# An attention and feed-forward kernel: an FFN step's activation one step later, weight loads behind queries, two banks for the values' products

## The chip, the cores and the metric

The kernel runs on one core of a Trainium2 chip. A core has five engines with queues of their own: TensorE (PE: matmuls, and PEld, the loading of the stationary operand), VectorE (DVE), ScalarE (ACT), GpSimd (POOL) and SyncE (SP, which only issues transfers here). Each engine takes its instructions in order and waits on semaphores. The metric is the device time of one execution in microseconds; the span in a profile is the time from the first to the last instruction of one profiled execution.

## The reference

```python
# q, k, v: 8 batches x 8 heads x 576 positions x 64
scores = scale * np.matmul(q, k.transpose(0, 1, 3, 2))
# heads 0..3: the last 32 positions; heads 4..7: equal position modulo 32, causal
scores = np.where(masks, scores, -1e9)
attn = np.exp(scores - scores.max(-1)); attn = attn / (attn.sum(-1) + 1e-9)
x = np.matmul(attn, v)           # regrouped to 4608 tokens x 512
h = x @ w_in                     # 512 x 2048
g = h * (1.0 / (1.0 + np.exp(-1.702 * h)))
return g @ w_out                 # 2048 x 512
```

## The kernel before

**Attention** goes in 48 pairs of blocks (`pairs`, l.50-71), four heads each. A pair's work: `scores` (PE), `maxima` (DVE), `softmax` (eight exponentials on ACT, the reciprocal of the sums on DVE, the scaling on POOL), a transposition, `values` (16 products on PE into one PSUM bank, then a high part by ACT and a low part by DVE, the tiles xh and xl). The first ten pairs (`n0`) are done ahead of the FFN in the loop of l.550-578; its turns are called stages here. Stage i has, in program order: scores(i+1) on PE, the load of q and k for pair i+3, the reciprocal of pair i-1, the fetch of the transposed pair i-2, the low part of pair i-3 and the maxima of pair i+1 on DVE, the exponentials of pair i on ACT, values(i-2) on PE with its high part on ACT, and PE's transposition of pair i-1. For these ten pairs all values' products go to one bank, `first_a` (l.145, l.293).

**The FFN** goes in 12 groups of 384 tokens and 16 slices f of 128 hidden units: 192 steps (`steps`, l.527), ordered (group 0, f 0-7), (group 1, f 0-15), (group 0, f 8-15), and then group by group. Step s has on PE `ffn1` (12 matmuls of 384 columns into a bank h), and at its end `ffn2` of step s-2 (9 matmuls of 512 columns into three banks o). Between them stands `act` (l.461): tanh on ACT, the product with h on DVE (both tile g), the high part gh on ACT, the low part gl on DVE. `ffn1` and `ffn2` take three products each, high x high, high x low and low x high, so that a weight's high and low parts are both needed.

**The weights** come as 64-bit words and are taken apart once, by a generator (`weights`, l.401); `weigh(n)` runs it until n turns, called beats here, have been issued. Per slice f of the weights: ACT scales the upper words (in the trace raw<-raw, f32) and makes the lower ones (raw<-raw, uint8), DVE joins them (raw<-raw, uint32); ACT then takes the high part (w<-raw) and DVE the low part (w<-raw,w). Beat 5+3f issues the joining of slice f+1 and the high part of f; beat 6+3f the low part of f, the load of slice f+4, and the scaling of f+2; beat 7+3f the lower words of f+2. The first four slices are loaded by explicit calls of `load_w`, two transfers of 512 KB each (l.533, l.554). Step s needs beats 5+3s and 6+3s.

**What sets the order.** PE keeps program order throughout. ACT, DVE, POOL and SP keep it as long as `strict` holds (l.600): until all 51 beats are issued, at step 21. After that a planner orders them by what is ready. PSUM has two banks for scores (`s`) and six for everything else (`x`, l.88): in the first stage four for scores and transpositions and one for the values, later three o, the banks h and one for values' products.

Of the kernel before, what the change touches and what calls it, by code (L numbers as in the profile page):

```python
# [43 lines left out]
LAG = 2  # L44
RAWB = 4
NH = NF // 2
WEIGHED = 6


def _pairs():  # L50

    def strided(b):
        return [("s", b, c) for c in range(0, len(RES), U)]

    def local(j):
        n = G // QL
        return [("l", i // NL, i % NL) for i in range(j * n, (j + 1) * n, U)]

    def weave(a, b):
        return [u for i in range(max(len(a), len(b))) for u in a[i : i + 1] + b[i : i + 1]]

    first = {}
    for b in range(B):
        first.setdefault(b * S // G, []).extend(strided(b))
    ahead = local(0) + first[0]
    windows = [weave(first.get(j + 1, []), local(j + 1)) for j in range(NG - 1)] + [[]]
    ahead += windows[0]
    windows[0] = []  # L70
    return ahead + [u for w in windows for u in w], windows, len(ahead)
# [3 lines left out]
def attn_ffn(ctx, tc, qk, vs, w_in, w_out, masks, ident, out):  # L75
# [11 lines left out]
    def bank(name):  # L87
        tag, n = ("s", 2) if name[0] == "s" else ("x", 6)
        return psum.tile([P, 512], F32, tag=tag, name=name, bufs=n)
# [7 lines left out]
    pairs, windows, n0 = _pairs()  # L97
# [32 lines left out]
    def load_v(p):  # L130
        if p < len(pairs) and p not in vts:
            vts[p] = io.tile([P, U, HEADS, D], F32, tag="v", name=f"v_{p}", bufs=2)
            sync.dma_start(out=vts[p], in_=vs[p])
# [8 lines left out]


    first = [[bank(f"{x}{j}") for j in range(2)] for x in "sut"]
    first_a = bank("a")


    prs = [const.tile([P, HU, P], F32, name=f"pr_{i}") for i in range(AHEAD)]
# [7 lines left out]
    def geom(p):  # L156

        kind, b, c = pairs[p]
        if kind == "l" and c == 0:
            m = masks_sb[:QL, 0:U].rearrange("p u n -> p (u n)")  # L160
            return QL, KL, m.unsqueeze(1).broadcast_to([QL, 2, U * KL])
        n, nk, i = (QL, KL, 1) if kind == "l" else (RES[c] * NPOS, RES[c] * NPOS, 2)
        return n, nk, masks_sb[:n, i, :nk].unsqueeze(1).broadcast_to([n, 2 * U, nk])
# [124 lines left out]
    def values(p):  # L288

        kind, b, c = pairs[p]  # L290
        nq, nk, _ = geom(p)
        v, pt = vts[p], pts[kind]
        ops = first_a if p < n0 else bank(f"a_{p}")
        for u in range(U):
            for g in range(2):
                for j in range(2):
                    i = g * U + u
                    matmul(
                        ops[j * D : (j + 1) * D, i * nq : (i + 1) * nq],
                        lhsT=v[:nk, u, 2 * g + j, :],  # L300
                        rhs=pt[:nk, j * 2 * U + i, :nq],
                        start=True,
                        stop=True,
                    )
        parts = []
        if kind == "l":
            j, o = divmod((NL * b + c) * QL, G)
            src = ops[:, : 2 * U * nq].rearrange("p (g n) -> p g n", g=2)
            parts.append([src] + [x[:, :, o : o + U * QL] for x in part("l", j)])
        else:  # L310
            n, r0 = U * RES[c], R0[c]
            src = ops[:, : 2 * U * nq].rearrange("p (g r t) -> p g t r", g=2, r=n)
            t0 = 0
            while t0 < NPOS:
                j, o = divmod(NPOS * b + t0, G // STRIDE)
                t1 = min(NPOS, t0 + G // STRIDE - o)
                xv = [x.rearrange("p c (t r) -> p c t r", r=STRIDE) for x in part("s", j)]
                parts.append(
                    [src[:, :, t0:t1]] + [x[:, :, o : o + t1 - t0, r0 : r0 + n] for x in xv]
                )  # L320
                t0 = t1
        yield
        for src, hi, _ in parts:
            scalar.copy(out=hi, in_=src)
        yield
        for src, hi, lo in parts:
            vector.tensor_tensor(out=lo, in0=src, in1=hi.bitcast(F32), op=ALU.subtract)
# [5 lines left out]
    def w_tile(shape, dtype, name):  # L333
        return wp.tile(shape, dtype, tag="w", name=name, bufs=NF)

    def load_w(f):

        if f >= NF:
            return
        raw = raws[f] = w_tile([P, 2, DM, 2], U32, f"raw_{f}")  # L340
        for m in range(2):
            sync.dma_start(out=raw[:, m], in_=(w_in, w_out)[m][f])
# [95 lines left out]
    made = [0]  # L438

    def weigh(n):  # L440

        while made[0] < n and next(wgen, 0) is None:
            made[0] += 1
# [17 lines left out]
    def act(j, f, beside=lambda: None):  # L461
        ps = hps.pop((j, f))
        g2 = ffn.tile([P, G], F32, tag="g2", name=f"g2_{j}_{f}", bufs=1)
        scalar.activation(g2, ps[:, :G], AF.Tanh, scale=0.851)
        vector.scalar_tensor_tensor(
            out=g2, in0=g2, scalar=1.0, in1=ps[:, :G], op0=ALU.add, op1=ALU.mult
        )
        beside()
        gh, gl = (
            ffn.tile([P, G], F32R, tag=f"g{x}", name=f"g{x}_{j}_{f}", bufs=LAG + 1) for x in "hl"  # L470
        )
        scalar.copy(out=gh, in_=g2)
        vector.tensor_tensor(out=gl, in0=g2, in1=gh.bitcast(F32), op=ALU.subtract)
        gs[j, f] = (gh, gl)
# [53 lines left out]
    steps = [(j, f) for j, f0, f1 in spans for f in range(f0, f1)]  # L528
# [1 line left out]
    load_v(0)  # L530
    ident_sb = const.tile([P, P], F32, name="ident_sb")
    sync.dma_start(out=ident_sb, in_=ident)
    load_w(0)
    scores(0)
    maxima(0)
    load_qk(2)
    load_v(1)
    halfway, valued = {}, {}

    def scaled(p):  # L540
        run(halfway.pop(p))
# [8 lines left out]
    for i in range(n0):  # L550
        if i + 1 < n0:
            scores(i + 1)
            load_qk(i + 3)
        if i + 1 < RAWB:
            load_w(i + 1)
        if i >= 1:
            scaled(i - 1)
        if i >= 2:
            fetch_pt(i - 2)
        if i >= 3:  # L560
            late_part(i - 3)
        if i + 1 < n0:
            maxima(i + 1)
        halfway[i] = softmax(i)
        run(halfway[i], 4)
        if i >= 2:
            value_products(i - 2)
            load_v(i)
            run(valued[i - 2], 1)
        weigh(i)  # L570
        if i == n0 - 2:
            turn_pr(i - 1)
            ffn1(*steps[0], (0, 1))
        elif i == n0 - 1:
            ffn1(*steps[0], (2, 3))
            turn_pr(i - 1)
        elif i >= 1:
            turn_pr(i - 1)
# [6 lines left out]
    p = n0  # L585
# [13 lines left out]
    for s in range(len(steps) + LAG):  # L599
        strict[0] = made[0] < 3 * NF + 3  # L600
        cur = steps[s] if s < len(steps) else None
        old = steps[s - LAG] if s >= LAG else None
        p, q, r = due.get(s), due.get(s - 1), begins.get(s)
        if cur:
            if s == 1:
                scaled(n0 - 1)
                fetch_pt(n0 - 2)
                late_part(n0 - 3)
            if s == 2:
                fetch_pt(n0 - 1)  # L610
                late_part(n0 - 2)
            if s > 0:
                ffn1(*cur, range(NC))
            if s in (1, 2):
                value_products(n0 - 3 + s)
            if s == 1:
                turn_pr(n0 - 1)
                act(*steps[0], lambda: weigh(made[0] + 1))
            goal = WEIGHED + min(3 * (s + 1), 3 * NH + (s + 1 - NH) * 3 // 2)
            if s > 0:  # L620
                act(*cur, lambda: weigh(min(made[0] + 1, goal)))
            if s in (1, 2):
                run(valued[n0 - 3 + s], 1)
            weigh(goal)
            if s == 2:
                late_part(n0 - 1)
        if late is not None:
            run(late[0], -(-4 // (late[1] - s)) if late[1] > s else HU)
        if p is not None:
            load_v(p)  # L630
            load_qk(p + AHEAD)
            transpose(p)
        if q is not None:
            run(values(q))
            load_v(q + 1)
        if r is not None:
            scores(r)
            maxima(r)
            load_qk(r + 1)
            if late is not None:  # L640
                run(late[0])
            late = softmax(r), turn[r]
            run(late[0], 1)
        if old:
            for parts in ((0, 1, 2),) if old[1] == NF - 1 else ((0, 1), (2,)):
                for i in range(NT):
                    ffn2(*old, i, parts)
            gs.pop(old)
# [77 lines left out]
```

## Time and profile before

| | us |
|---|---|
| median of three runs | 962.55 (960.97 to 963.12) |
| the profiled execution | 961.34 |
| its span | 959.6 |
| PE busy | 930.5 |
| DVE busy | 523.3 |
| ACT busy | 408.7 |

Two runs of the same kernel differ here by up to 2.2 us. In the views below a row of the timeline has start, duration, engine, line, operation, tiles out<-in and the shapes; in square brackets stands how long the engine sat idle before it and what ended that. All work is issued through one helper, so every line is L108, and one goes by tile names: s, u scores; t transposed; a values' products; h, o, g, gh, gl the FFN; raw, w the weights; qk, v queries with keys, and values.

### The profile page before, as it was taken

What the parts mean: (1) busy time and instruction counts of PE and PEld (TensorE: products, weight loads), DVE (VectorE), ACT (ScalarE), POOL (GpSimd) and SP (SyncE); (2) the same over time, 40 slices, a digit from 0 to 9 for tenths busy, and PEclk for the clock granted to TensorE, in tenths of its full rate; (3) what the DMA queues carried; (4) which work ended last, traced back from release to release, by engine and by line L of the source; (5) the groups of instructions that cost most, each with busy time, mean ns of one, the idle gap of its engine ahead of it and who ended that gap; (6) DMA issues with size and microseconds to landing.
All of it is one profiled execution on the core that took longest, in us unless ns stands there. A gap on an engine that the chain in (4) does not pass through costs nothing.

```text
span 959.6 us, 14692 instructions
## 1 busy us (share of the span) xinstructions
PE 930.5 (97%) x5668; PEld 818.8 (85%) x5668; DVE 523.3 (55%) x999; ACT 408.7 (43%) x1289; POOL 85.7 (9%) x56
## 2 busy tenths in 40 slices
PE   7786999999999999999999999999999999999997
PEld 5665889888888888898888888888888888888996
DVE  4765557566656564545665655453656675422322
ACT  6865665334444442423434343332443434222221
POOL 3310001011010110000101010000110101000000
PEclk9889999999999999999999999999999999999999
DMA  8764201213213121102222211111121210000000
GB/s 325 247 216 186 88 23 66 67 33 100 67 33 99 35 66 44 56 1 67 66 64 70 65 35 55 45 34 45 54 67 34 100 44 12 33 1 1 33 1 33
DMA packets 24374, 65.10 MB, mean 68 GB/s; under 512 B 2672, under 2 KB 3440, under 8 KB 24304
## 3 DMA queue, kind: packets, MB, share of 16 engines
q1 hardware_dynamic: 24304, 64.17, 20.0%
q8 instruction: 44, 0.72, 0.3%
q14 instruction: 26, 0.21, 0.1%
HBM read 54.72 MB, written 9.44 MB: 67 GB/s over the span
## 4 chain that ended last, share of the span: by engine, by line
PE 93%; DVE 3%; ACT 2%; DMA 1%; issue 1%; SPq 0%; ACTq 0%; DVEq 0%
PE h L108 42%; PE o L108 42%; PE s L108 5%; PE a L108 4%; DMA qk<-qk 1%; DVE raw L108 1%; DVE w L108 1%; ACT raw L108 1%; PE t L108 1%; ACT pr L108 1%; ACT g L108 0%; ACT gh L108 0%; DVE nmax L108 0%; ACT w L108 0%; PE u L108 0%
## 5 line engine op out<-in xcount | busy, mean ns | idle before, releaser
L108 PE MATMUL o<-w,gh 128*128 128x512 f32 x1152 | 308.4, 400 | 0.0
L108 PEld LDWEIGHTS o<-w,gh 128*128 128x128 f32 x1152 | 211.6, 188 | 40.2 <-issue 0.2
L108 PE MATMUL h<-xhl,w 128*128 128x384 f32 x768 | 233.0, 344 | 11.6 <-DVE w L108 7.1
L108 PE MATMUL h<-xhs,w 128*128 128x384 f32 x768 | 227.7, 337 | 0.0
L108 DVE SCALAR_TENSOR_TENSOR g<-g,h 128x384 f32<-128x384 f32 x192 | 106.4, 554 | 206.1 <-ACT g L108 205.0
L108 ACT ACTIVATE g<-h 128x384 f32<-128x384 f32 x192 | 93.6, 488 | 270.6 <-PE h L108 202.0
L108 DVE TENSOR_TENSOR gl<-g,gh 128x384 fp32r<-128x384 f32 x192 | 127.1, 662 | 82.4 <-ACT gh L108 81.2
L108 PE MATMUL o<-w,gl 128*128 128x512 f32 x576 | 169.4, 395 | 0.0
L108 PEld LDWEIGHTS h<-xhl,w 128*128 128x128 f32 x768 | 141.6, 188 | 24.0 <-DVE w L108 9.0
L108 ACT ACTIVATE pr<-pr,nmax 96x128 f32<-96x128 f32 (+2 forms) x304 | 114.1, 377 | 107.2 <-DVE nmax L108 106.7
L108 ACT CAST gh<-g 128x384 fp32r<-128x384 f32 x192 | 98.8, 514 | 130.9 <-DVE g L108 130.8
L108 POOL TENSOR_TENSOR pr<-pr,rinv 96x1024 f32<-96x1024 f32 (+2 forms) x48 | 82.1, 1710 | 726.3 <-DVE rinv L108 726.3
L108 PEld LDWEIGHTS h<-xhs,w 128*128 128x128 f32 x768 | 142.6, 189 | 0.1
L108 PEld LDWEIGHTS o<-w,gl 128*128 128x128 f32 x576 | 108.2, 188 | 26.0
L108 PE MATMUL h<-xll,w 128*128 128x384 f32 x384 | 130.1, 339 | 0.0
L108 PE MATMUL h<-xls,w 128*128 128x384 f32 x384 | 129.0, 336 | 0.0
L108 PEld LDWEIGHTS h<-xll,w 128*128 128x128 f32 x384 | 72.3, 188 | 8.3
L108 PEld LDWEIGHTS h<-xls,w 128*128 128x128 f32 x384 | 72.7, 189 | 0.0
L108 DVE TENSOR_SCALAR rinv<-ssum 96x8 f32<-96x8 f32 (+2 forms) x48 | 8.0, 167 | 93.3 <-ACT pr L108 93.0
L108 ACT ACTIVATION_READ_ACCUMULATOR pr<-pr,nmax 96x1 f32 (+2 forms) x304 | 56.9, 187 | 0.0
L108 DVE STREAM_TRANSPOSE pt_l<-pr 32x256 f32<-32x256 f32 x120 | 52.1, 434 | 3.3 <-POOL pr L108 1.9
L108 PE MATMUL s<-qk 64*96 64x128 f32 (+2 forms) x688 | 46.8, 278 | 1.8 <-DMA qk<-qk 1.8
(52 smaller groups left out, 544.6 us busy)
## 6 DMA issues: line engine op xcount, KB each, us to landing
qk<-qk SPq DMA_DIRECT2D x47, 512.0 KB, 4.1
v<-vs SPq DMA_DIRECT2D x48, 256.0 KB, 2.8
out<-out SPq DMA_DIRECT2D x36, 256.0 KB, 2.8
raw<-w_in SPq DMA_DIRECT2D x16, 512.0 KB, 4.8
raw<-w_out SPq DMA_DIRECT2D x16, 512.0 KB, 6.3
qk<-qk SPq DMA_DIRECT2D x2, 256.0 KB, 3.2
masks_sb<-masks SPq DMA_DIRECT2D x1, 128.0 KB, 2.1
ident_sb<-ident SPq DMA_DIRECT2D x1, 64.0 KB, 5.4
```

The costliest lines, as they stand in the source:

```text
L108: ins = call(*args, **kw)
```

## The change

- `act` of step s-1 is issued in step s, after `ffn1` of step s; before it was issued in step s itself. Step 1 issues one `act` and not two, and the last is issued at step 192.
- The beats run one ahead: stage i has issued i+1 of them (none at stage 0, two at stage 1), and `WEIGHED` is 7.
- The first weights' load stands behind the load of q and k of pair 2 and of v of pair 1; the next three come in stages 1, 3 and 5 (before: 0, 1 and 2), behind that stage's q, k and v.
- The values' products of pairs 0 to 6 alternate between two banks; pairs 7, 8 and 9 use the first. The second is bank number six, which h of step 0 takes over.

```diff
-WEIGHED = 6
+WEIGHED = 7
...
-    first_a = bank("a")
+    first_a = [bank(f"a{j}") for j in range(2)]
...
-        ops = first_a if p < n0 else bank(f"a_{p}")
+        ops = first_a[p % 2 if p < n0 - 3 else 0] if p < n0 else bank(f"a_{p}")
...
-    load_w(0)
     scores(0)
     maxima(0)
     load_qk(2)
     load_v(1)
+    load_w(0)
...
-        if i + 1 < RAWB:
-            load_w(i + 1)
...
-        weigh(i)
+        if i % 2 and i // 2 + 1 < RAWB:
+            load_w(i // 2 + 1)
+        weigh(i and i + 1)
...
-                act(*steps[0], lambda: weigh(made[0] + 1))
+        if 0 < s <= len(steps):
             goal = WEIGHED + min(3 * (s + 1), 3 * NH + (s + 1 - NH) * 3 // 2)
-            if s > 0:
-                act(*cur, lambda: weigh(min(made[0] + 1, goal)))
+            act(*steps[s - 1], lambda: weigh(min(made[0] + 1, goal)))
             if s in (1, 2):
                 run(valued[n0 - 3 + s], 1)
             weigh(goal)
```

## The prediction

> **What bounds the kernel now.** I read first the busy time in stretches, then PE's waits, then the chain that ended last, then one step in order of time. The stretches (length, then busy time and instructions of PE, PEld, DVE, ACT, POOL, then PE's granted clock):
>
> ```profile
> 8.00:53.00 45.00, 36.20 (x376) 29.11 (x377) 32.45 (x81) 39.60 (x182) 15.48 (x10) 0.92 0.80 289
> 53.00:101.00 48.00, 36.42 (x178) 29.34 (x177) 24.65 (x36) 28.04 (x40) 0.92 (x1) 0.89 0.54 206
> 101.00:955.00 854.00, 853.73 (x5098) 758.17 (x5096) 464.19 (x880) 339.60 (x1067) 65.69 (x38) 1.00 0.15 47
> ```
>
> From 101 us on PE is the bound: idle for 0.27 us of 854, at full clock. No edit takes a matmul away, so nothing is to be won there. What can be won lies ahead of 101 us: the first ten pairs (8 to 53), where ACT is the fullest engine, and the first FFN steps (53 to 101), where PE loses 11.6 us to waits and more to a clock of 0.89. PE's waits in that second stretch, and the chain of all work with the starts of four `ffn1`:
>
> ```profile
> PE h L108 <- DVE w L108: 7.1, 6, 1.7
> PE h L108 <- ACT w L108: 4.5, 5, 1.1
> ```
> ```profile
> 59.65 3.58 PE h L108 x10
> ...
> 100.91 2.11 PE h L108 x12
> 105.11 2.11 PE h L108 x12
> 109.32 2.11 PE h L108 x12
> ```
>
> At full pace a step takes PE 109.32 - 105.11 = 4.21 us. The 59.65 is `ffn1` of step 2 (its last ten matmuls) and the 100.91 that of step 8, the first whose weights were ready long before. So six steps took 41.26 us. Why, one step in order of time shows, ACT, then DVE, then PE:
>
> ```profile
> 91.95 0.49 ACT L108 ACTIVATE g<-h 128x384 f32<-128x384 f32 x1 [2.89 <-PE h L108]
> 92.34 1.14 ACT L108 ACTIVATE raw<-raw 128x1024 uint32<-128x1024 uint8 x1
> 93.36 0.51 ACT L108 CAST gh<-g 128x384 fp32r<-128x384 f32 x1
> 93.76 1.12 ACT L108 CAST w<-raw 128x1024 fp32r<-128x1024 f32 x1
> 94.78 1.18 ACT L108 ACTIVATE raw<-raw 128x1024 f32<-128x1024 f32 x1
> 98.85 0.49 ACT L108 ACTIVATE g<-h 128x384 f32<-128x384 f32 x1 [2.88 <-PE h L108]
> ```
> ```profile
> 92.48 0.55 DVE L108 SCALAR_TENSOR_TENSOR g<-g,h 128x384 f32<-128x384 f32 x1 [2.62 <-ACT g L108]
> 93.90 0.56 DVE L108 TENSOR_TENSOR gl<-g,gh 128x384 fp32r<-128x384 f32 x1 [0.87 <-ACT gh L108]
> 94.38 1.22 DVE L108 SCALAR_TENSOR_TENSOR raw<-raw 128x1024 uint32<-128x1024 uint32 x1
> 95.51 1.22 DVE L108 TENSOR_TENSOR w<-raw,w 128x1024 fp32r<-128x1024 f32 x1
> ```
> ```profile
> 94.94 0.44 PE L108 MATMUL h<-xhl,w 128*128 128x384 f32 x1 [0.92 <-ACT w L108]
> 96.79 0.61 PE L108 MATMUL h<-xhl,w 128*128 128x384 f32 x2 [1.23 <-DVE w L108]
> ```
>
> The reader is to see a ring. ACT's queue holds tanh ahead of the weights' work, so ACT sits idle for 2.89 us until PE has ended `ffn1`. Only then come the lower words, gh, gl, the joining, the weights' low part (ends 96.73), and PE goes on at 96.79 with the next `ffn1`, whose end lets the next tanh start at 98.85. One turn is 98.85 - 91.95 = 6.90 us where PE needs 4.21.
>
> **Part 1, the activation one step later (the largest term).** In step s the queues now hold tanh(s-1), whose h was ended a step ago, so nothing in them waits for the running `ffn1`. No instruction is added; per step, ACT issues tanh, a weight's high part, gh, scaling, lower words. From start to start the rows above give 0.39 + 1.02 + 0.40 + 1.02, and the scaling's 1.18 less about 0.13 of overlap: 3.88 us. DVE: g and gl 0.48 each, joining and low part 1.13 each: 3.2. Both are below PE's 4.21. The order inside a step: tanh at 0, high part from 0.4 to 1.5, gh to 2.0, while DVE does g to 1.05, joins to 2.2, gl to 2.7, the low part to 3.8. So weights for step s+1 are there 3.8 us after tanh(s-1) starts. The ring still closes, but over two steps: 3.8 plus `ffn1` 2.11 is 5.9 us per two steps against PE's 8.4. What is late next is nothing: PE.
>
> What PE then needs from the third matmul of step 2 to step 8 is 6 x 4.21, less 0.35 for the two matmuls before, plus the values' products of pair 9, 0.84 at full clock by this row:
>
> ```profile
> 49.80 0.84 PE L108 MATMUL a<-pt_s,v 90*64 90x90 f32 x16 [1.35 <-DVE xll L108]
> ```
>
> That is 25.75 us. I allow 0.3 for step 3, where DVE still has pair 9's transposed copy and pair 8's low part ahead of the weights. 41.26 - 26.05 = **15.2 us**. If every step instead cost the sum of ACT's durations with the gaps of today's queue, see the rivals.
>
> Behind step 8 the later `act` costs nothing as long as ACT and DVE stay below PE; they are at 40% and 54% in the long stretch. In an order kept by the program they run ahead until tanh waits for its own h again, as now. A second h bank is held: three o, two h and one for values make the six there are. Below zero or above it I see no reason for more than some tenths; the last steps (`act` issued at step 192) have 4.2 us of `ffn2` as cover.
>
> **Part 2, how the FFN begins.** Stage 9's last beat and the rows that follow:
>
> ```profile
> 52.08 1.23 ACT L108 ACTIVATE raw<-raw 128x1024 f32<-128x1024 f32 x1
> ...
> 58.38 1.22 DVE L108 TENSOR_TENSOR w<-raw,w 128x1024 fp32r<-128x1024 f32 x1
> ```
>
> ACT ends the stages at 53.31; the third matmul of step 2 came 6.34 us later, because step 1 held two `act` with the weights between and behind them. Now it holds one. DVE has the fetch of pair 8 and pair 7's low part first (I take them to end 1.0 after ACT), then g 0.55, joining 1.13, gl 0.48, low part 1.22: about 4.5. Gain **1.8 us**. PE has `ffn1` of step 1, pair 8's values and pair 9's transposition to fill it, and waits about 1 us.
>
> **Part 3, loads and beats in the stages.** ACT's waits between 8 and 53 us; then three transfers with their time to landing (q and k of pair 2 issued at 6.54, v of pair 2 at 19.71, the second half of slice 0 at 4.58), and PE standing still for two of them:
>
> ```profile
> ACT pr L108 <- DVE nmax L108: 5.9, 1, 5.9
> ACT xhs L108 <- PE a L108: 3.2, 2, 2.3
> ACT pr L108 <- DVE rinv L108: 1.2, 2, 0.9
> ACT xhl L108 <- PE a L108: 0.8, 1, 0.8
> ```
> ```profile
> qk<-qk SPq DMA_DIRECT2D x1, 512.0 KB, 6.3
> v<-vs SPq DMA_DIRECT2D x1, 256.0 KB, 8.4
> raw<-w_out SPq DMA_DIRECT2D x1, 512.0 KB, 6.9
> ```
> ```profile
> 12.88 1.78 PE L108 MATMUL s<-qk 64*108 64x108 f32 x16 [1.32 <-DMA qk<-qk]
> ...
> 28.26 1.71 PE L108 MATMUL a<-pt_s,v 108*64 108x108 f32 x16 [2.25 <-DVE rinv L108]
> ```
>
> The 5.9 is the start, before the first exponentials; no edit touches it. The other 5.2 us are what ACT loses. The values' products at 28.26 are put down to DVE, but v of pair 2 lands at 19.71 + 8.4 = 28.1, just ahead of them: I take it for the load, stuck among the weights. At 12.88 it is pair 2's queries that come late. With the first slice behind pair 2's queries and the others two stages apart, v and queries land in about the time of quiet ones, and the two waits for values' products, 2.3 and 0.9, go. I leave 1.0 of the 5.2, since pair 1's scores and the first values still arrive late for other reasons. Against it stands one more beat inside the stages, about 1.0 (its later place is in part 2). Gain 5.2 - 1.0 - 1.0 = **3.2 us**; both ends: 4.2 if no wait is left, 0 if the weights come too late (rival 2). The loads have no buffer to wait for; on SP they now stand behind q, k and v, whose waits they share: the second slice's load behind pair 4's, which waits for scores(2).
>
> **Part 4, two banks.** The wait of 1.35 in the row at 49.80 (pair 7 waits for pair 6's low part) stays, as those share the first bank; the like waits of pairs 4 to 6 go. Cost and gain nothing: there ACT, 39.6 of 45 us busy, is behind every stage, and PE's time is its cover. `ffn1` of step 0 now waits for pair 5's low part, done a stage earlier.
>
> **A rule about the clock.** Two microseconds behind the wait at 28.26, the third number from the right being the granted clock:
>
> ```profile
> 28.00:30.00 2.00, 1.74 (x17) 1.51 (x18) 0.17 (x1) 0.00 (x0) 1.39 (x1) 0.50 0.47 178
> ```
>
> A wait of 2.25 us was enough to halve it. The Trainium skill, "TensorE: Matmul & The Clock Gate", Part 1, says the clock halves after at least one idle window of about 3.4 us; by that this one would not have come, so the trace differs, and the sum below, which has no dip, would be certain of that term. By the rows it is not: the ten matmuls at 59.65, behind waits no longer than 1.7 us, took 3.58 us, where twelve take 2.11 at full clock, or 1.76 for ten. A dip behind part 2's wait of about 1 us would cost some 1.8 us; I leave it out of the sum and keep it in the range.
>
> **The sum.** 15.2 + 1.8 + 3.2 = 20.2 us. The profiled span 959.6 becomes 939.4, its execution 961.3 becomes 941.1; the median shown is 1.2 above that execution, so 962.55 becomes **942.3 us**.
>
> **The rivals.**
> 1. ACT takes over the steps. If high part, gh and scaling keep the stalls between them, a step costs the durations' sum, 4.44, and about 0.4 of waiting on DVE: 4.85. Six steps lose 3.9 us: 946. For it: 3.88 against 4.21 leaves little. Against it: the rows' starts overlap already.
> 2. Weights too late. The scaling of slices 0 and 1 as it stands now:
>
> ```profile
> 14.63 1.18 ACT L108 ACTIVATE raw<-raw 128x1024 f32<-128x1024 f32 x1
> ...
> 23.99 1.18 ACT L108 ACTIVATE raw<-raw 128x1024 f32<-128x1024 f32 x1
> ```
>
> Slice 0 will be issued about 1.3 us behind 6.54; at 6.9 us it lands at 14.7, where ACT, less held up by scores, wants it at about 13.9. Slice 1 is wanted a stage earlier than now, (23.99 - 14.63) / 2 = 4.7 us, at 19.3; issued behind scores(2), near 13.4, it lands at 21.8 if it takes the 8.4 above. ACT keeps order, so 0.8 + 2.5 = 3.3 us stand in the exponentials' way and part 3 gives nothing: 945.5. With rival 1: 949. [...]
> 3. Slower: banks. If in the 38 steps with a later pair's values `ffn1` must wait for the second h bank, because exponentials stand ahead of tanh in ACT's queue: eight are at most (39.6 - 9 x 1.18) / 10 = 2.9 us, with tanh and DVE's g 3.9, less 2.1 of `ffn2`: 1.8 each, 38 x 1.8 = 68, so 1010. It decides from 20.2 / 38 = 0.53 us per such step. For it: six banks are exactly filled. Against it: ACT and DVE are half idle there, and the planner may take tanh first once the weights are done.
> 4. The change does nothing: the planner orders the early steps as before, 962. Against it: program order is kept up to step 21.
>
> **How the numbers follow.** Forecast (939 to 944.5) 0.52; rival 1 or 2 alone (944.5 to 948) 0.25; both, or with a dip (948 to 953) 0.11; lower than 939, 0.02; rival 4 and other no change 0.03; rival 3 0.07. A difference of 0.2%, 1.9 us, is about what a measurement of this kernel can tell from none. Faster 0.90, same 0.03, slower 0.07. The range 938.8 to 951 leaves out some 0.15.
>
> **What would show it.** Right: in the changed profile a step of PE from step 3 on takes 4.2 us, the waits of PE h for w fall from 11.6 to about 1, ACT's tanh no longer shows idle time there, the long stretch starts near 81 us. Part 3 is right if ACT ends the stages near 50. Wrong: ACT waiting for raw from a DMA before 25 us (rival 2), steps of 4.5 or more (rival 1), or any wait of PE in the long stretch (rival 3).

## The result and the profile after

The changed kernel takes 940.63 us (median of four runs, 940.31 to 941.84); the kernel before, on the same chip, 962.69 us. The ratio is 0.9776 with a 95% interval of 0.9759 to 0.9793: 22.1 us faster. The profiled execution took 941.84 us, with a span of 940.1 us; that is the highest of the four.

First the stretches of the changed kernel's profile (the columns as in the prediction):

```profile
53.00:80.00 27.00, 26.60 (x163) 23.51 (x162) 23.82 (x34) 26.14 (x36) 0.00 (x0) 1.00 0.82 304
80.00:101.00 21.00, 21.00 (x107) 18.97 (x106) 12.65 (x18) 13.95 (x21) 0.00 (x0) 1.00 0.22 87
101.00:935.00 834.00, 834.00 (x5000) 740.64 (x4999) 448.95 (x861) 324.43 (x1046) 65.67 (x38) 1.00 0.15 47
```

From 53 us on PE idles for 0.40 us, at full clock; before, the stretch from 53 to 101 us had 11.6 us of idle time at a clock of 0.89. That 0.40 us is one wait, the only one left of PE h for w:

```profile
PE h L108 <- DVE w L108: 0.4, 1, 0.4
```

The chain of all work, with the starts of `ffn1` of steps 2 (its last ten matmuls), 3, 4 and 8:

```profile
56.42 2.01 PE h L108 x10
...
61.50 2.11 PE h L108 x12
...
65.71 2.11 PE h L108 x12
...
82.54 2.11 PE h L108 x12
```

Step 3 to step 4 is 4.21 us. From the third matmul of step 2 to step 8 it is 82.54 - 56.42 = 26.12 us, where it was 41.26. One step in order of time, ACT and then DVE, shows the ring open:

```profile
65.64 0.48 ACT L108 ACTIVATE g<-h 128x384 f32<-128x384 f32 x1
66.01 1.13 ACT L108 CAST w<-raw 128x1024 fp32r<-128x1024 f32 x1
67.05 0.51 ACT L108 CAST gh<-g 128x384 fp32r<-128x384 f32 x1
67.46 2.18 ACT L108 ACTIVATE raw<-raw 128x1024 f32<-128x1024 f32 x2
69.53 0.49 ACT L108 ACTIVATE g<-h 128x384 f32<-128x384 f32 x1
```
```profile
66.16 0.55 DVE L108 SCALAR_TENSOR_TENSOR g<-g,h 128x384 f32<-128x384 f32 x1 [0.61 <-ACT g L108]
66.63 1.22 DVE L108 SCALAR_TENSOR_TENSOR raw<-raw 128x1024 uint32<-128x1024 uint32 x1
67.76 0.55 DVE L108 TENSOR_TENSOR gl<-g,gh 128x384 fp32r<-128x384 f32 x1
68.23 1.22 DVE L108 TENSOR_TENSOR w<-raw,w 128x1024 fp32r<-128x1024 f32 x1
```

No ACT row has idle time ahead of it. ACT turns in 69.53 - 65.64 = 3.89 us, less than PE's 4.21; the weights' low part for the next step ends at 69.45, and the next `ffn1` is not due before 69.92.

The stages are another matter. Rows of ACT (the first exponentials; the scaling of slice 1; a high part of values; the last beat), then of PE (the second half of the first scores; scores of pair 9), then a transfer with its time to landing (q and k of pair 9, issued at 34.57):

```profile
9.57 0.36 ACT L108 ACTIVATE pr<-s,nmax 96x128 f32<-96x128 f32 x1 [7.34 <-DVE nmax L108]
...
21.62 1.17 ACT L108 ACTIVATE raw<-raw 128x1024 f32<-128x1024 f32 x1 [0.67 <-DMA raw<-w_out]
...
46.68 0.48 ACT L108 CAST xhl<-a 128x384 fp32r<-128x384 f32 x1 [0.93 <-PE a L108]
...
51.00 1.16 ACT L108 ACTIVATE raw<-raw 128x1024 uint32<-128x1024 uint8 x1
```
```profile
6.75 1.17 PE L108 MATMUL s<-qk 64*96 64x128 f32 x8 [1.16 <-DMA qk<-qk]
...
43.63 1.53 PE L108 MATMUL u<-qk 64*90 64x90 f32 x16 [1.76 <-DMA qk<-qk]
```
```profile
qk<-qk SPq DMA_DIRECT2D x1, 512.0 KB, 9.0
```

ACT ends the stages at 52.16, where 53.31 stood before and 50.1 was expected. It began 1.46 us later (9.57 against 8.11), behind first scores that stood 1.16 us waiting for queries and keys; it waited for a weight's slice, and for values behind scores whose queries took 9.0 us to land.

The two spans differ by 19.5 us: the end of the stages gives 53.31 - 52.16 = 1.15; the way from there to step 2's third matmul 6.34 - 4.26 = 2.08; the way on to step 8 gives 15.14; and what lies behind step 8's start 858.7 - 857.6 = 1.1. That last one is no work of the loop: over all later steps the starts of `ffn2` stand 18.37 us earlier in the changed kernel, each of them within 0.01, and the last stores land 2 us after issue in both. What fills the 1.1 us behind them the profile doesn't show.

### The profile page after: what moved, and what is told of

Its sections match the earlier page's. It is cut to its first block, busy times and chain, and to the rows that moved or that the text cites. A ratio compares the mean times of both kernels' runs of the same rounds, so it can differ in the third digit from the quotient of the medians.

```text
span 940.1 us, 14682 instructions
## 1 busy us (share of the span) xinstructions
PE 924.2 (98%) x5668; PEld 815.1 (87%) x5668; DVE 520.3 (55%) x999; ACT 408.0 (43%) x1289; POOL 85.7 (9%) x56
## 4 chain that ended last, share of the span: by engine, by line
PE 95%; DVE 2%; DMA 1%; ACT 1%; issue 0%; POOL 0%; SPq 0%; ACTq 0%; POOLq 0%
PE o L108 44%; PE h L108 43%; PE s L108 4%; PE a L108 4%; DMA qk<-qk 1%; ACT pr L108 1%; PE u L108 1%; DVE nmax L108 0%; PE t L108 0%; DVE w L108 0%; DVE raw L108 0%; POOL pr L108 0%; DVE pt_l L108 0%; ACT raw L108 0%; SPq L108 0%
```

## The experiments

Theory: the ring through tanh held the first steps at 6.9 us each, and opening it gives about 15 us, the earlier loads some 3 more, and the beat ahead and the single `act` of step 1 some 2 more. Rivals: the loads, or the clock they spare, carry the gain; the beats ahead carry it; ACT replaces the ring as the bound of the steps.

All are timed beside the kernel before on the same chip; there it measured 960.33 us in the first group of four (11 runs, 957.0 to 964.4), 960.35 in the second and 960.65 in the third. "Stages' end" is the end of ACT's last beat ahead of the first tanh; the next columns are the starts of step 2's third matmul and of step 8, from the chain of each profile (for old_loads and act_more, step 2 from PE's timeline).

| kernel | median us | ratio to before, 95% | stages' end | step 2 | step 8 |
|---|---|---|---|---|---|
| lag_only | 945.35 | 0.9848 (0.9816, 0.9881) | 51.85 | 56.95 | 83.86 |
| no_lag | 950.08 | 0.9891 (0.9864, 0.9919) | 50.04 | 55.46 | 89.18 |
| old_loads | 942.38 | 0.9811 (0.9784, 0.9839) | 52.50 | 57.55 | 83.99 |
| one_bank | 941.41 | 0.9801 (0.9775, 0.9827) | 50.95 | 54.91 | 81.03 |
| again | 940.22 | 0.9788 (0.9775, 0.9802) | 50.11 | 54.30 | 80.44 |
| not_ahead | 942.98 | 0.9815 (0.9800, 0.9829) | 49.57 | 54.70 | 83.10 |
| even | 939.77 | 0.9789 (0.9774, 0.9805) | 50.09 | 53.99 | 80.10 |
| act_more | 944.51 | 0.9837 (0.9823, 0.9850) | 50.34 | 55.18 | 85.21 |
| again_b | 940.95 | 0.9797 (0.9773, 0.9821) | 50.22 | 55.00 | 81.11 |
| loads_only | 956.96 | 0.9957 (0.9939, 0.9976) | 49.91 | 56.26 | 96.22 |
| pool_high | 941.50 | 0.9796 (0.9771, 0.9821) | 51.82 | 56.48 | 82.59 |
| pool_even | 939.19 | 0.9784 (0.9761, 0.9806) | 51.51 | 56.29 | 82.41 |

### The later activation alone (lag_only)

On the kernel before:

```diff
-                act(*steps[0], lambda: weigh(made[0] + 1))
+        if 0 < s <= len(steps):
             goal = WEIGHED + min(...)
-            if s > 0:
-                act(*cur, lambda: weigh(min(made[0] + 1, goal)))
+            act(*steps[s - 1], lambda: weigh(min(made[0] + 1, goal)))
```

> The kernel before with the later activation alone (loads, beats and banks as before). If the ring through tanh is the cause: weights for step s+1 come 4.8 us after the tanh of step s-1, steps 3 to 7 cost PE 4.2 us each, and from the stages' end (53.3) it is 5.2 us to the third matmul of step 2 and 26.1 from there to step 8, which starts near 84.6 instead of 100.9: about 946.4 us. If the loads or the clock carried the gain: 958 or more. PE's waits for w about 1.5 us instead of 11.6.

Measured 945.35 us, 15.0 below the kernel before. PE's waits for weights, and the chain's starts of steps 2 and 8:

```profile
PE h L108 <- DVE w L108: 0.9, 2, 0.6
PE h L108 <- ACT w L108: 0.9, 1, 0.9
```
```profile
56.95 2.01 PE h L108 x10
...
83.86 2.11 PE h L108 x12
```

The waits are 1.8 us in place of 11.6, and step 2 to step 8 takes 26.91 us in place of 41.26, with the loads, beats and bank of the kernel before. One edit gives three quarters of the gain; the loads are not its cause.

### Everything but the later activation (no_lag)

The reverse of that diff, on the changed kernel.

> The changed kernel with each activation in its own step again (loads, beats one ahead and two banks kept). Ring: the beat between tanh and gh is now the weight's high part and the joining, so tanh 0.5, g 0.55, joining 1.15, gl 0.5, low part 1.2 and ten matmuls 1.8 give about 5.8 us per step against 4.2: six steps lose 10 us, and step 1 with two activations loses 1 more: about 951.5. If the later activation is worth nothing once the beats run ahead: 941. If the whole old ring is back (6.9 per step): 957.

Measured 950.08 us. Waits of PE; two starts of `ffn2`; and tanh's row:

```profile
PE h L108 <- DVE w L108: 7.9, 6, 1.6
```
```profile
75.08 1.56 PE L108 MATMUL o<-w,gh 128*128 128x512 f32 x6
...
81.00 1.33 PE L108 MATMUL o<-w,gh 128*128 128x512 f32 x5
```
```profile
81.20 0.49 ACT L108 ACTIVATE g<-h 128x384 f32<-128x384 f32 x1 [1.92 <-PE h L108]
```

A step is 5.92 us: the beat ahead takes one operation out of the ring (6.9 before), but it stays closed, and ACT again sits 1.92 us ahead of tanh. Added to the kernel before, the later activation is worth 15 us; taken from the changed one, 9 to 10, since the beat ahead shortens the ring it would leave. One thing more stands in this profile: PE waits 1.46 us in each of these steps, and yet from 8 us on the granted clock never falls to a half, as it does twice in the first steps of the kernel before. So waits like the ring's do not bring the lower clock every time.

### Loads: the old ones back, and the new ones alone (old_loads, loads_only)

```diff
+    load_w(0)
     scores(0)
...
-    load_w(0)
...
+        if i + 1 < RAWB:
+            load_w(i + 1)
...
-        if i % 2 and i // 2 + 1 < RAWB:
-            load_w(i // 2 + 1)
```

loads_only puts the new places into the kernel before, the reverse of this.

> The changed kernel with the first four weights' loads at their old places. If part 3 of the prediction holds: values of pair 2 land late again, ACT loses 2 to 3 us in the stages, 943 to 943.5. If only the small waits differ (in the changed profile ACT still lost 2.0 us to loads): 940.6 to 941.5.

> The kernel before with the loads of the first four weights in their new places, and nothing else. If part 3 holds, pair 2's values land in time, ACT ends its stages up to 4 us earlier (49 to 51; there is no tenth beat), and the old steps follow unchanged: 3 to 4 us below the kernel before. If the first steps take up what the stages gain: no difference.

With the old places the changed kernel measured 942.38 us, some 1 to 2 us above itself, with intervals that overlap. That lies between the two ranges expected (940.6 to 941.5, and 943 to 943.5) and decides for neither. Its waits (PE, then ACT):

```profile
PE a L108 <- DMA v<-vs: 2.3, 1, 2.3
```
```profile
ACT xhs L108 <- PE a L108: 3.1, 2, 2.4
```

This stands where the wait of 2.25 us stood that the profile of before put down to DVE, ahead of the values' products of pair 2. Here it carries its own name: the load of values. With the new places alone, in the kernel before, both rows are gone. The stages end at 49.91. That is 3.4 us earlier than in the profile of before, but only 1.9 earlier than in that of lag_only (51.85), whose stages are the same program as those of before. The whole is 3.7 us faster, while PE still waits for weights as ever:

```profile
PE h L108 <- DVE w L108: 7.4, 6, 1.7
PE h L108 <- ACT w L108: 5.2, 6, 1.0
```

So the first steps did not take up what the stages gained: from the stages' end to step 2's third matmul it is 6.35 us, where it was 6.34.

How much of the 3.7 us is the wait itself is open. In all three profiles with the old places (before, lag_only, old_loads) the clock stands at a half for some us behind it, between 28 and 34 us. Among runs whose mean granted clock was 0.998 the two kernels lie closer: 955.0 to 957.6 with the new places and 957.0 to 957.7 with the old, three runs each.

### One bank (one_bank)

```diff
-        ops = first_a[p % 2 if p < n0 - 3 else 0] if p < n0 else bank(f"a_{p}")
+        ops = first_a[0] if p < n0 else bank(f"a_{p}")
```

> The changed kernel with one bank for the values' products of the first ten pairs. If ACT is behind every stage and PE's waits have cover: 940.6 to 941.2, with waits of PE a for DVE xls of some 3 us in all in the stages. If values' products are on the path: each of some six waits of 1 us counts, 943 or more.

Measured 941.41 us: no difference from the changed kernel that these runs can tell. PE's waits for the bank are there as expected, 5.0 us of them:

```profile
PE a L108 <- DVE xll L108: 2.6, 3, 1.2
PE a L108 <- DVE xls L108: 2.4, 3, 1.1
```

### The changed kernel again, and the beats not ahead (again, again_b, not_ahead)

```diff
-WEIGHED = 7
+WEIGHED = 6
...
-        weigh(i and i + 1)
+        weigh(i)
```

> The changed kernel once more, beside the next three on the same chip: 940 to 942. If the 9.57 us of the first exponentials in its first profile (8.11 before) came with the change, they start near 9.5 again; if it was that run's transfer alone, between 8.1 and 8.8, as in the other profiles.

> The changed kernel, third time, as the base for the next three on the same chip: 940 to 942.

> The changed kernel with the beats not ahead (stage i has issued i of them, the rest one later). ACT ends the stages 1.0 us earlier, but the third matmul of step 2 then comes 5.2 us behind that and not 4.3: no difference, 940 to 942, if a beat is only moved from one side of the stages' end to the other. If running ahead is what frees PE: steps 2 and 3 wait for w, 943 or more.

Again: 940.22 and 940.95 us. The first exponentials and the last beat of the second profile:

```profile
8.17 0.36 ACT L108 ACTIVATE pr<-s,nmax 96x128 f32<-96x128 f32 x1 [5.94 <-DVE nmax L108]
...
48.89 1.22 ACT L108 ACTIVATE raw<-raw 128x1024 uint32<-128x1024 uint8 x1
```

They start at 8.17 (8.46 in the third), so the 9.57 came with that execution's first transfers and not with the change; not_ahead has a like start, 9.17. The stages end at 50.11 and 50.22, as forecast. Steps 2 to 8 take 26.14 and 26.11 us.

Without the beat ahead the kernel measured 942.98 us, 2.8 above the changed kernel on that chip, though the intervals just touch (0.9800 and 0.9802). The expectation of no difference (940 to 942) fell. In its profile the stages do end earlier, at 49.57, and step 2's third matmul follows 5.13 us later as expected; but step 3 waits as well:

```profile
PE h L108 <- ACT w L108: 0.9, 1, 0.9
PE h L108 <- DVE w L108: 0.9, 2, 0.6
```
```profile
54.70 3.00 PE h L108 x10
```

The ten matmuls of step 2 took 3.00 us and not 2.0: behind these waits the clock was halved for a while (0.50 between 56 and 58 us). From there to step 8 it is 28.40 us. lag_only has the same waits without that dip in the clock and takes 26.91, the changed kernel 26.12; so in this one profile about 0.8 us goes to the waits and 1.5 to the clock. How the 2.8 us between the medians divide stays open.

### More work for ACT in each step (act_more)

```diff
         scalar.activation(g2, ps[:, :G], AF.Tanh, scale=0.851)
+        if (j, f) in steps[:7]:
+            scalar.activation(g2, ps[:, :G], AF.Tanh, scale=0.851)
...
         scalar.copy(out=gh, in_=g2)
+        if (j, f) in steps[:7]:
+            scalar.copy(out=gh, in_=g2)
```

> The changed kernel with tanh and gh issued twice each in the activations of steps 0 to 6, so 0.8 us more of ACT per step. If ACT's 3.9 us per step have only 0.3 of cover under PE's 4.2: steps of 4.7 us from step 2 on, 0.8 us at step 1 and about 0.45 for each of six steps: 944 to 945. If ACT has more cover than that: 941. If the ring is still closed over one step: 0.8 for each step, 947.

Measured 944.51 us. ACT's tanh in two steps, and PE's waits:

```profile
71.38 1.01 ACT L108 ACTIVATE g<-h 128x384 f32<-128x384 f32 x2
...
76.33 1.01 ACT L108 ACTIVATE g<-h 128x384 f32<-128x384 f32 x2
```
```profile
PE h L108 <- DVE w L108: 3.1, 6, 0.9
```

A step is 4.95 us: 1.06 more than ACT's 3.89, since the doubled tanh and gh took 0.90 and 0.96 us up to the next start, 0.53 and 0.55 more than single ones. PE follows ACT one to one. ACT's margin under PE was 0.3 us per step, and not more: the changed kernel's steps are held by PE, with ACT close behind.

### Less work for ACT in the stages; loads one stage earlier (pool_high, even, pool_even)

```diff
-                scalar.copy(out=hi, in_=v)
+                if f < 2:
+                    gpsimd.tensor_copy(out=hi, in_=v)
+                else:
+                    scalar.copy(out=hi, in_=v)
```

```diff
-        if i % 2 and i // 2 + 1 < RAWB:
+        if i % 2 == 0 and i // 2 + 1 < RAWB:
```

> The changed kernel with the high parts of the first two weights' slices made by GpSimd and not by ACT (two instructions of 1.03 us in ACT's queue, stages 4 and 7). If ACT is what paces the stages, they end 2 us earlier and the whole is 2 us shorter than the changed kernel: 938.5. If DVE or PE paces them as much: 940.5. If GpSimd's copy takes so long that the scaling of the probabilities queues behind it: 942 or more.

> The changed kernel with the loads of weights 1, 2 and 3 in stages 0, 2 and 4 (not 1, 3 and 5). In the changed profile ACT waited 0.7 us for slice 1 and PE 1.8 us for the queries of pair 9, which came behind slices 3 and 4 issued together. If these waits are on the path: ACT's wait for raw goes below 0.5, and 1 us is won, 939.5. If other transfers then come late: 941 or more.

> The same with the loads of weights 1, 2 and 3 in stages 0, 2 and 4: 0 to 1 us below the kernel with GpSimd's high parts alone, 938; equal to it if the loads' places make no difference.

With GpSimd's high parts: 941.50 us, no gain. GpSimd's copy is no slower than ACT's; ACT's wait for values and the wait of PE behind it took the room:

```profile
26.78 1.12 POOL L108 CAST w<-raw 128x1024 fp32r<-128x1024 f32 x1
```
```profile
ACT xhl L108 <- PE a L108: 3.8, 2, 3.0
```
```profile
43.25 1.53 PE L108 MATMUL u<-qk 64*90 64x90 f32 x16 [2.86 <-DMA qk<-qk]
```

ACT has 2 us less to do and the stages end no earlier (51.82). The queries of pair 9 come late once more, as in the first profile of the changed kernel. With the loads one stage earlier (even) ACT no longer waits for a weight and PE waits 0.6 us for the queries of pair 9, but the time, 939.77 us, can't be told from 940.22; both edits together give 939.19, with an interval (0.9761 to 0.9806) that covers the changed kernel's. No version here is shown to beat it.

## Why the prediction was right

**The sum.** 942.3 us was forecast and 940.63 measured; the gain was to be 20.2 us and is 22.1 in the runs of the result, 20.1 and 19.7 in the two later groups where the changed kernel ran. The changed kernel is the same everywhere (940.2 to 941.0); it is the kernel before that measured 962.7 beside the result and 960.3 to 960.7 in the later groups.

**Part 1, 15.2 us.** 15.14 in the profile, and what was said of the changed kernel holds at each step: ACT's turn of 3.88 us is 3.89, the stretch of 26.05 us with its allowance is 26.12, 26.14 and 26.11 in three profiles. Taken alone it gave 15.0 us with part of part 2 in it. What it was subtracted from was read too simply. The 41.26 us is near six turns of 6.90 by accident: from step 2's third matmul to step 8 there are five turns and a last piece of 100.91 - 96.79 = 4.12, 38.6 us in all. The other 2.6 is clock, as the chain of the kernel before shows, with the ten matmuls of steps 3, 4 and 5:

```profile
68.06 2.04 PE h L108 x10
...
74.96 3.22 PE h L108 x10
...
83.03 2.02 PE h L108 x10
```

Ten matmuls took 3.58 us in step 2 and 3.22 in step 4, with a granted clock of 0.50 from 60 to 64 and from 76 to 78 us, and about 2.0 in the other steps. loads_only has the same ring with one such stretch (3.46 us in step 2), and takes 96.22 - 56.26 = 39.96. So of the 15.14 us the open ring gives 12.5, and 2.6 is a lower clock that did not recur there. The forecast named the clock of 0.89 and then gave it no term of its own; that its total came out owes something to the luck of the execution profiled. Some runs of the kernel before kept a mean granted clock of 0.998: 957.0 to 957.7 us, some 16.5 above the changed kernel and not 20.

**Part 2, 1.8 us.** 2.08 in the first profile: 4.26 us from the stages' end against the 4.5 forecast, 4.19 and 4.78 in the next two. The reason was half named. The prediction put it to the single `act` of step 1; with that alone (lag_only) it is 56.95 - 51.85 = 5.10 us, and with everything but the beat ahead (not_ahead) 5.13. The rest comes with the beat ahead, whose other half the prediction counted as a loss of 1.0 in part 3.

**Part 3, 3.2 us.** In the first profile 1.15: ACT started 1.46 us late there, and the 0.6 still missing is less than its waits for weights (1.1) and values (0.9). In the two others it is 3.2 and 3.1. All three are measured from one profile of the kernel before, and the same stages end 1.46 us earlier in lag_only; by that one the gain is 1.6 to 1.7. So the size of part 3 is known to no better than 1.5 us. The load of values as the cause of the 2.25 us is shown by old_loads, which names it, and by loads_only, where it goes once the weights' loads are moved. Of ACT's waits the prediction left 1.0 us over; 1.6 remain in the second profile.

**Part 4, nothing.** Right as measured; the cover given for it was too simple. That ACT is "behind every stage" fell with pool_high: with 2 us less on ACT the stages end no earlier, since loads of queries and PE's products stand right behind it. Why taking 2 us away gains nothing, while the waits of the loads did gain, is argued from one profile each. That it gains nothing doesn't hang on the clock: the one run of each at a mean clock of 1.000 took 939.67 us with GpSimd's high parts and 939.77 without.

**The rivals.** Rival 1 did not come, but by 0.3 us per step only, as act_more shows. Rival 2 came in small: ACT waited 1.1 us for weights in the first profile, 0.2 in the second and 0.7 in the third, where 3.3 were bounded. Slice 0 landed at 15.7 and at 14.0 us in the first two, against the 14.7 forecast. Rival 3 did not: PE is busy 834.00 of 834 us behind 101. Rival 4 did not either: the first steps changed.

**The clock.** In the changed kernel it stayed at 1.00 from 53 us on, so the dip kept in the range for part 2's wait did not come. Its price was set too high: at full clock ten matmuls take 2.04 us (at 68.06, above) and not 1.76, so it would be some 1.5 us. A dip came once in the stages, behind the wait for pair 9's queries:

```profile
44.00:46.00 2.00, 2.00 (x28) 1.84 (x28) 0.81 (x2) 1.76 (x11) 0.00 (x0) 0.50 0.29 106
```

That wait was 1.76 us. It is again shorter than the idle window of about 3.4 us that the Trainium skill, "TensorE: Matmul & The Clock Gate", Part 1, gives for the halving, so the trace differs here too. What sets off the dip isn't shown: in the second profile the clock stood at a half from 33.8 to 40.8 us, and PE's longest wait in the seven us before was 0.81.

## What to carry to other kernels

Where an engine's queue holds the consumer of the running step ahead of the producer for the next one, the step becomes a ring, and its length is the sum round it, however idle each engine looks. Issue the consumer one step later and the ring closes over two steps; then the longest single queue counts, so add up each engine's starts and see how far it is below the next bound. Add up the old stretch as well, turn by turn: where the number of turns times one turn gives its length only by accident, something else, here the clock, makes up the rest. Bulk loads that nobody needs for a while cost time where they stand ahead of small ones that somebody waits for.

## What was not expected

- One kernel's runs spread differently: the kernel before over 7 us (957.0 to 964.4 in 11 runs), the changed one over 3 (939.7 to 942.8 in 13). The profile of the first has three stretches at half clock; the changed kernel's have one each, at about 43 to 47, 34 to 41 and 44 to 48 us. The mean granted clock that the record has for each run goes with the time: in those 11 runs of the kernel before it falls from 0.998 at 957.0 us to 0.987 at 964.4; the 13 of the changed kernel all have 0.996 or more. That the lower clock makes the spread, and doesn't merely come with longer waits, is not shown.
- The engine that a profile names for a wait can change where the wait does not: with the loads at the same old places, the 2.3 us ahead of pair 2's values' products stood as DVE in before and in lag_only, and as the load of values in old_loads.
- GpSimd's conversion of 128x1024 took 1.12 us, as short as ACT's 1.16.
